# A two-branch layer kernel: the next block's x loads issued two phase rotations sooner

**Chip, cores, metric.** One core of a Trainium2 chip. The experiments ran in five rounds on five chips (the record numbers them 0, 6, 8, 9 and 12); ratios compare kernels within a round. The metric is device microseconds (us) of one execution, median of several runs; lower is better.

## The reference, cut

`out = x + A(layernorm(x)) + B(layernorm(x))` for 2048 rows of 1024 numbers in bfloat16. A is a linear recurrence over the rows with complex states; B is a dense layer of width 3584 with the activation `h * tanh(softplus(h))` between two matrix products.

```python
    x = A_x
    xn = _layernorm(x, axis=-1)
    return x + _A_ref(xn, ...) + _B_ref(xn, B_w1, B_b1, B_w2)   # arguments cut
```

## The kernel before

The rows go through in four blocks of 512. In each block the TensorE makes 28 tiles of the first dense layer (one PSUM bank each, eight banks in turn), then eight pairs of projections into the recurrence, then the tail (the second dense layer and the recurrence's output). The weights pass through a ring of SBUF slots, which SyncE refills in pairs. The VectorE copies each tile out of its bank and does, in the same in-order queue, everything else that is small: among it, in the first block, the layer norm statistics of the *next* block. In the first block GpSimd also makes the phases of the rotation table, eight rotations of three operations. The next block's x is loaded by GpSimd from the middle of these.

```python
    def load_x(queue, blk, q):                      # 128 rows, 256 KB
        r0 = blk * TB + q * P
        i = blk % 2
        queue.dma(lambda e: e.dma_start(xx[:, i, q, :], A_x[0, r0:r0 + P, :]), ...)   # cut

    def ln_stats_only(blk, q):                      # VectorE; waits for the load
        ...
            vop(lambda e, h=h: e.bn_stats(stats[:, s, h, :], xx[:, i, q, h * 512:(h + 1) * 512]), ...)
        vop(lambda e: e.bn_aggr(mv[:, q, :], stats[:, s, :, :]), ...)

    for j in range(NJ):                             # GpSimd
        phases(j)                                   # rotation j: px, py, ph
        if j == 3:
            for q in range(NQ):
                load_x(PO, 1, q)

    def first_tile(blk, f):
        bank, hs = f % 8, f % (2 * GF)
        ...                                         # 8 matmuls into the bank; weights from the ring
        if f % 4 == 3:
            item_done()                             # SyncE loads two more ring slots
            item_done()
        if f % GF == 0 and f >= 2 * GF:
            mish_mul(f // GF - 2)                   # VectorE group multiply, at f = 14 and 21
        vop(lambda e: e.tensor_scalar(hb[:, hs, ts], ps[:, bank, ts], b1(f), None, op0=ALU.add), ...)

        def side(f):                                # after first_tile(blk, f); here the first block
            ...                                     # cut
            if f in (14, 16, 18, 20):
                ln_stats_only(1, (f - 14) // 2)
            if f < 24 and f % 3 == 2:
                transpose_B(f // 3)                 # SyncE, the same in-order queue as the ring
```

Of the kernel before, what the change touches and what calls it, by code (L numbers as in the profile page):

```python
# [135 lines left out]
def bass_parallel_sum__ssm_conv_s5__dense_activation_mish__prompt_kernel(  # L136
    nc: bass.Bass,
    A_x: bass.AP,
    A_Lambda_re: bass.AP,
    A_Lambda_im: bass.AP,  # L140
    A_B_re: bass.AP,
    A_B_im: bass.AP,
    A_C_re: bass.AP,
    A_C_im: bass.AP,
    A_log_dt: bass.AP,
    A_Dskip: bass.AP,
    B_x: bass.AP,
    B_w1: bass.AP,
    B_b1: bass.AP,
    B_w2: bass.AP,  # L150
    out: bass.AP,
):
    build_kernel(nc, A_x, A_Lambda_re, A_Lambda_im, A_B_re, A_B_im, A_C_re, A_C_im,
                 A_log_dt, A_Dskip, B_w1, B_b1, B_w2, out)


def build_kernel(nc, A_x, A_Lambda_re, A_Lambda_im, A_B_re, A_B_im, A_C_re, A_C_im,
# [149 lines left out]
    def load_x(queue, blk, q):  # L307
        r0 = blk * TB + q * P
        i = blk % 2
        queue.dma(lambda e: e.dma_start(xx[:, i, q, :], A_x[0, r0:r0 + P, :]),  # L310
                  s_xx[i][q] if blk else s_x0[q], writes=[b_xx[i][q]])
# [310 lines left out]
    def phases(j):  # L622

        xs, b_xs = ph_slot(j)
        pop(lambda e: e.tensor_scalar(px[:], iot[:], cj("thp", j), None, op0=ALU.mult),  # L625
            reads=[b_iot, b_cs["thp"]], writes=[b_px])
        pop(lambda e: e.tensor_scalar(py[:], px[:], ROUND_MAGIC, -ROUND_MAGIC, op0=ALU.add, op1=ALU.add),  # L627
            reads=[b_px], writes=[b_py])
        pop(lambda e: e.tensor_tensor(xs[:], px[:], py[:], op=ALU.subtract),  # L629
            reads=[b_px, b_py], writes=[b_xs])  # L630
# [45 lines left out]
    turns()  # L676
    for j in range(NJ):
        phases(j)
        if j == 3:
            for q in range(NQ):  # L680
                load_x(PO, 1, q)

# [299 lines left out]
```

## Time and profile before

| | before |
|---|---|
| timed, first set of runs | 620.77 us (620.40 to 621.11) |
| the profiled execution | 623.69 us, span 622.4 us |
| TensorE | 99% busy |
| VectorE, ScalarE, GpSimd | 75%, 40%, 9% |

The table by stretches of this profile says where the TensorE is idle. Its columns are the stretch, its length, then busy us (and instructions) of TensorE, weight loads, VectorE, ScalarE and GpSimd, the granted clock, the DMA share and GB/s.

```profile
0.00:22.24 22.24, 20.46 (x194) 17.90 (x194) 16.45 (x49) 9.40 (x17) 8.15 (x22) 1.00 0.98 258
22.24:60.55 38.31, 38.30 (x178) 17.02 (x175) 34.12 (x66) 32.85 (x23) 36.47 (x26) 1.00 1.08 270
60.55:62.35 1.80, 0.00 (x1) 0.01 (x1) 1.69 (x3) 1.77 (x3) 1.80 (x1) 1.00 1.30 331
```

Two places: some 1.8 us in the start, which the change doesn't touch, and one stop of 1.80 us in which the VectorE is the one that works. The DMA engines are full (share about 1) in all three.

### The profile page before, as it was taken

Reading aid. Unit: us, or ns where it says so; the run is one execution under the profiler, and the core shown is the slowest. Engines: PE = TensorE matmul, PEld = TensorE weight load, DVE = VectorE, ACT = ScalarE, POOL = GpSimd, SP = SyncE. Lnnn points to the kernel's source line nnn. Section 1 sums busy time; section 2 is a strip of 40 time slices with the busy share of each in tenths; the row PEclk is TensorE's granted clock in tenths of the full one; section 3 lists DMA queues with packets and bytes.
Section 4 is the critical chain, followed back from the end, with each engine's and each line's share of the span. In section 5 each row is a group of like instructions: output and inputs, shape, how many; then the busy total and the mean of one; then the engine's idle time right before and its main releaser. Section 6 shows DMA issues by size and latency. Waiting matters only on the chain.

```text
span 622.4 us, 7428 instructions
## 1 busy us (share of the span) xinstructions
PE 616.7 (99%) x2959; PEld 288.3 (46%) x2959; DVE 468.1 (75%) x698; ACT 248.1 (40%) x161; POOL 54.5 (9%) x57
## 2 busy tenths in 40 slices
PE   8998999999999999999999999999999999999998
PEld 7643444444444444444444444444444444444444
DVE  6988999999557599999047759999624856999603
ACT  4589997332069950000008992000000999000000
POOL 2899200000100000000010000000000000000000
DMA  9999995850355400774054430276302541033001
GB/s 230 298 263 280 224 145 176 199 167 0 117 173 174 144 2 9 218 185 131 11 188 138 135 136 1 73 203 173 93 35 101 164 174 69 1 119 118 1 0 68
DMA packets 97918, 79.94 MB, mean 128 GB/s; under 512 B 51035, under 2 KB 80347, under 8 KB 97883
## 3 DMA queue, kind: packets, MB, share of 16 engines
q1 hardware_dynamic: 94384, 72.17, 41.4%
q0 software_dynamic: 960, 3.15, 1.8%
q10 hardware_dynamic: 2538, 4.14, 1.8%
q8 instruction: 24, 0.39, 0.3%
q14 instruction: 12, 0.09, 0.1%
HBM read 63.19 MB, written 4.19 MB: 108 GB/s over the span
## 4 chain that ended last, share of the span: by engine, by line
PE 90%; POOL 4%; DMA 2%; DVE 2%; issue 1%; SPq 0%; POOLq 0%; DVEq 0%
PE ps L825 49%; PE ps L745 23%; PE ps L767 18%; DMA xx<-in_A_x_dram 2%; POOL py L627 1%; POOL px L625 1%; POOL ph_h L629 1%; DVE stats L449 1%; POOL rb L568 1%; DVE hb L754 1%; DVE act L730 0%; PE ps L839 0%; DVE stats L371 0%; SPq L310 0%; SPq L343 0%
## 5 line engine op out<-in xcount | busy, mean ns | idle before, releaser
L825 PE MATMUL ps<-ring,act 128*128 128x512 bf16 x896 | 194.0, 379 | 0.0
L745 PE MATMUL ps<-xnT,ring 128*128 128x512 bf16 x840 | 182.1, 379 | 0.0
L723 ACT ACTIVATE act<-hb 128x3584 bf16<-128x3584 bf16 x16 | 50.9, 3183 | 220.6 <-DVE hb L754 220.1
L825 PEld LDWEIGHTS ps<-ring,act 128*128 128x128 bf16 x896 | 87.7, 98 | 105.7
L745 PEld LDWEIGHTS ps<-xnT,ring 128*128 128x128 bf16 x840 | 82.1, 98 | 99.2 <-DVE hb L754 0.7
L754 DVE TENSOR_SCALAR hb<-ps,par 128x512 bf16<-128x512 f32 (+1 forms) x112 | 80.0, 730 | 52.6 <-PE ps L745 51.7
L767 PE MATMUL ps<-xnT,BT 128*128 128x512 bf16 x512 | 111.3, 379 | 1.8 <-DVE hb L754 1.8
L825 PE MATMUL ps<-CT,hT 128*128 128x512 bf16 x506 | 109.9, 379 | 0.0
L772 DVE TENSOR_TENSOR mt<-ps,tab 128x1024 bf16<-128x1024 f32 x64 | 75.4, 1219 | 13.3 <-PE ps L767 11.7
L767 PEld LDWEIGHTS ps<-xnT,BT 128*128 128x128 bf16 x512 | 50.0, 98 | 62.5 <-DVE hb L754 2.3
L825 PEld LDWEIGHTS ps<-CT,hT 128*128 128x128 bf16 x506 | 49.5, 98 | 59.7
L790 DVE TENSOR_TENSOR_SCAN hT<-cs,qi,hT 128x512 bf16<-128x512 f32 x48 | 58.9, 1269 | 0.0
L870 DVE TENSOR_TENSOR xx<-ps,xx 128x1024 bf16<-128x1024 f32 (+1 forms) x16 | 18.8, 1190 | 45.6 <-PE ps L825 45.6
L725 ACT ACTIVATE act<-act 128x3584 bf16<-128x3584 bf16 x16 | 51.1, 3191 | 0.2
L724 ACT ACTIVATE act<-act 128x3584 bf16<-128x3584 bf16 x16 | 51.0, 3190 | 0.2
L795 DVE TENSOR_TENSOR mt<-hT,tab 128x1024 bf16<-128x1024 bf16 x64 | 41.4, 688 | 1.1
L730 DVE TENSOR_TENSOR act<-act,hb 128x3584 bf16<-128x3584 bf16 x16 | 34.0, 2127 | 1.3 <-ACT act L725 1.3
L310 POOL DMA_DIRECT2D xx<-in_A_x_dram x12 | 6.7, 562 | 250.2 <-DVE xx L870 245.8
L699 ACT ACTIVATE ct<-CT,cs 128x512 f32<-128x512 bf16 x16 | 11.5, 720 | 26.3 <-DVE CT L701 25.9
L725 ACT ACT_TABLE_LOAD x16 | 20.5, 1283 | 0.3
L724 ACT ACT_TABLE_LOAD x16 | 20.5, 1283 | 0.3
L449 DVE BATCH_NORM_STATS2 stats<-xx 128x6 f32<-128x512 bf16 x24 | 16.3, 679 | 3.7 <-DMA xx<-in_A_x_dram 3.3
(101 smaller groups left out, 297.9 us busy)
## 6 DMA issues: line engine op xcount, KB each, us to landing
ring<-in_B_w_dram SPq DMA_DIRECT2D x112, 512.0 KB, 4.1
out_dram<-xx ACTq DMA_DIRECT2D x15, 256.0 KB, 2.0
xx<-in_A_x_dram POOLq DMA_DIRECT2D x12, 256.0 KB, 4.2
xx<-in_A_x_dram SPq DMA_DIRECT2D x3, 256.0 KB, 4.7
xx<-in_A_x_dram SPq DMA_DIRECT2D x2, 128.0 KB, 2.3
dsk<-in_A_Dskip_dram SPq DMA_DIRECT2D x1, 256.0 KB, 5.1
xnT<-xn SPq DMA_TRANSPOSE x14, 4.5
BT<-in_A_B_re_dram SPq DMA_TRANSPOSE x8, 5.8
```

The lines of the kernel that those rows point to most:

```text
L449: vop(lambda e, h=h: e.bn_stats(stats[:, s, h, :], xx[:, i, q, h * 512:(h + 1) * 512]), reads=[b_xx[i][q]], writes=[b_stats[s]])
L723: aop(lambda e: e.activation(a, hs, AF.Exp), reads=[b_hb[g % 2]], writes=[b_act[g]])
L724: aop(lambda e: e.activation(a, a, AF.Ln, bias=1.0), reads=[b_act[g]], writes=[b_act[g]])
L725: aop(lambda e: e.activation(a, a, AF.Tanh), reads=[b_act[g]], writes=[b_act[g]])
L730: vop(lambda e: e.tensor_tensor(a, a, hs, op=ALU.mult), reads=[b_act[g], b_hb[g % 2]], writes=[b_act[g]])
L745: PE.mm(lambda e, k=k, w=w: e.matmul(ps[:, bank, :], lhsT=w, rhs=xnT[:, k, :], start=k == 0, stop=k == NK - 1), reads=[b_ring[s]] + b_xnT, ...
L754: vop(lambda e: e.tensor_scalar(hb[:, hs, ts], ps[:, bank, ts], b1(f), None, op0=ALU.add), reads=[b_ps[bank], b_par], writes=[b_hbf[hs]])
L767: PE.mm(lambda e, j=j, ci=ci, k=k, bank=bank: e.matmul(ps[:, bank + ci, :], lhsT=BT[:, ci, j, k, :], rhs=xnT[:, k, :], start=k == 0, stop= ...
L772: vop(lambda e, s=s, u=u, j=j: e.tensor_tensor(mt[:, s, :, :], u, tab[:, s, j, :].unsqueeze(1).to_broadcast([P, 2, TB]), op=ALU.mult), rea ...
L790: vop(lambda e, ci=ci, init=init: e.tensor_tensor_scan(out=hT[:, ci, j, :], data0=cj("r", j).to_broadcast([P, TB]), data1=hT[:, ci, j, :], ...
L795: vop(lambda e, s=s: e.tensor_tensor(mt[:, s, :, :], hT[:, :, j, :], tab[:, s, j, :].unsqueeze(1).to_broadcast([P, 2, TB]), op=ALU.mult), ...
L825: PE.mm(lambda e: e.matmul(ps[:, u, :], lhsT=lhsT, rhs=rhs, start=st_, stop=last), reads=reads, writes=[b_ps[u]], first=st_, last=last)
```

## The change

Its intent: x of the next block lands before the VectorE asks for it, so that the VectorE never waits and frees the PSUM banks in time.

```diff
     for j in range(NJ):
         phases(j)
-        if j == 3:
+        if j == 1:
             for q in range(NQ):
                 load_x(PO, 1, q)
```

## The prediction

> **What bounds the kernel now.** I read the page first, for the bound and for the chain of waits; then the timeline of the TensorE around the first block, to find where it really stands still; then the timeline of the VectorE back from that stop, and the GpSimd's timeline and the DMA issues for what set off the wait.
>
> ```profile
> PE 616.7 (99%) x2959; PEld 288.3 (46%) x2959; DVE 468.1 (75%) x698; ACT 248.1 (40%) x161; POOL 54.5 (9%) x57
> ...
> PE 90%; POOL 4%; DMA 2%; DVE 2%; issue 1%; SPq 0%; POOLq 0%; DVEq 0%
> ```
>
> The TensorE is busy for 616.7 of 622.4 us, so all its idle time together is 5.7 us. The chain gives 4% to GpSimd and 2% to DMA, some 37 us, but that is not what a change there can win: the chain only says whom the last released instruction waited for, and while it runs through GpSimd and a transfer the TensorE is still working. What can be won is the time in which the TensorE stands still:
>
> ```profile
> 22.24 36.58 PE L745 MATMUL ps<-xnT,ring 128*128 128x512 bf16 x168
> 58.66 1.89 PE L767 MATMUL ps<-xnT,BT 128*128 128x512 bf16 x8
> 62.35 7.94 PE L767 MATMUL ps<-xnT,BT 128*128 128x512 bf16 x36 [1.80 <-DVE hb L754]
> ```
>
> 168 matmuls in 36.42 us are 217 ns each, and in the later stages the chain has 352 in 75.97 us, 216 ns each: the TensorE runs at its full pace up to 60.55 us, stops once for 1.80 us, and runs through to the end. In the list of waits from 22 to 64 us that is its only matmul wait; the weight loads have 0.7 us more in two waits for the same VectorE line. The stop is for a PSUM bank: the second projection tile writes bank 5, which tile 21 of the first layer used, and the VectorE has not copied tile 21 out. Why it is late stands in its timeline:
>
> ```profile
> 41.33 2.71 DVE L730 TENSOR_TENSOR act<-act,hb 128x3584 bf16<-128x3584 bf16 x1
> 44.14 0.75 DVE L754 TENSOR_SCALAR hb<-ps,par 128x512 bf16<-128x512 f32 x1
> 47.41 1.43 DVE L449 BATCH_NORM_STATS2 stats<-xx 128x6 f32<-128x512 bf16 x2 [2.51 <-DMA xx<-in_A_x_dram]
> 48.87 0.21 DVE L451 BATCH_NORM_AGGREGATE mv<-stats 128x2 f32<-128x12 f32 x1
> 48.99 1.36 DVE L754 TENSOR_SCALAR hb<-ps,par 128x512 bf16<-128x512 f32 x2
> 51.12 1.42 DVE L449 BATCH_NORM_STATS2 stats<-xx 128x6 f32<-128x512 bf16 x2 [0.78 <-DMA xx<-in_A_x_dram]
> ...
> 58.40 3.03 DVE L730 TENSOR_TENSOR act<-act,hb 128x3584 bf16<-128x3584 bf16 x1
> 61.54 2.07 DVE L754 TENSOR_SCALAR hb<-ps,par 128x512 bf16<-128x512 f32 x3
> ```
>
> The VectorE takes its work in order. After tile 14 it wants the statistics of the next block's x, whose first two quarters have not landed: it waits 2.51 and 0.78 us, 3.29 us together. Apart from that it is full. Tile 21 comes out of its copy at 62.30 us; the TensorE wanted the bank at 60.55. The x loads are late because GpSimd issues them only after four phase rotations:
>
> ```profile
> 31.41 1.57 POOL L625 TENSOR_SCALAR px<-iot,cs 128x512 f32<-128x512 f32 x1
> ...
> 40.89 1.27 POOL L629 TENSOR_TENSOR ph_h<-px,py 128x512 f32<-128x512 f32 x1
> 42.10 2.35 POOL L310 DMA_DIRECT2D xx<-in_A_x_dram  x4
> ```
>
> The listing of that load's line in this stretch gives 5.3 us from issue to landing for the first, then 8.3, 8.7 and 8.9 us. The DMA engines are full meanwhile: the table by stretches has a DMA share of 1.09 from 31.31 to 42.10 us, 1.09 to 53.98 and 1.11 to 62.35.
>
> **What the Trainium skill says.** "SBUF — State Buffer", section "Who interferes with whom": VectorE and GpSimd share a port pair that one instruction holds for its whole length, and a VectorE instruction with two SBUF inputs contends with a GpSimd instruction that reads SBUF. The trace agrees in kind: the 128x3584 multiply takes 2.71 and 3.03 us beside GpSimd and 2.02 us at 92.20, where GpSimd is done. The same page, "A bandwidth-pool intuition that's wrong (but worth ruling out)", warns that a load issued by GpSimd can lack its descriptors while the VectorE holds that pair. Here the issues took 0.54 to 0.75 us each although the multiply ran from 41.33 to 44.04, so no such starvation shows. "DMA: Bandwidth & Descriptors", section "Anatomy of one DMA — SWDGE (gpsimd) path", fits 2.0 us plus bytes/436e3 for such a load: 2.6 us for 256 KB. The trace has 5.3 to 8.9 us, so here the queueing behind weights and transposes decides; the measurement stands. The same page, "Issuing engines are not separate DMA queues", says all issuers share 16 DMA engines: the loads will not be free at their new place either.
>
> **The change part by part.** No instruction is added or removed. Four issues (2.35 us of GpSimd) move ahead of phase rotations 2 and 3.
>
> Loads: the second rotation ends at 31.31 us, so the issues lie at about 31.4 to 33.7 instead of 42.1 to 44.4, 10.8 us earlier. With the same transfer times of 5.3 to 8.9 us they land at about 36.7 to 42 us; double the longest and the last is there at about 51. The VectorE asks for the quarters at 44.9, and, without waits, at about 48, 51 and 53.7. All of its 3.29 us of waiting go.
>
> GpSimd: rotations 2 and 3 end 2.35 us later, at about 38.9 and 44.5; from the fifth on nothing moves, since the same work lies before it. ScalarE reads rotation 2 at 59.0 and rotation 3 at 61.05. This costs nothing.
>
> VectorE: tile 14 is out at 44.89. Then statistics and tiles follow without a gap, and the multiply moves from 58.40 to 58.40 − 3.29 = 55.1 us. It needs the tanh of its group, which ScalarE ends at 53.64: still 1.5 us of room. Tile 21 is out at 62.30 − 3.29 = 59.0 us. The TensorE wants its bank at 60.55: 1.5 us of room. The stop of 1.80 us is gone, and half of what the VectorE gains is slack.
>
> Behind it: the first projection result is read by the VectorE after tile 27, at 66.15 − 3.29 = 62.9, when the TensorE ends it at about 62.1 and its table is long there (57.1). ScalarE's activations keep their times, because they wait for each other and not for x: the last tanh of this block ends at 96.88. The multiply behind it, at 98.51 now, can move up only to that, about 1.6 us. So the VectorE keeps 1.6 us of its 3.29 there while the TensorE runs 1.8 us earlier. That 0.2 us comes out of the slack before the last part of the block: the last scaled C rows are ready at 156.4 us, and their first use is 16 matmuls before the tail's end at 164.39, at about 160.9, so 4.5 us. From the second block on, everything hangs on the TensorE and moves with it.
>
> Sum: −1.80 us, and perhaps −0.2 us more from the two weight-load waits. 620.77 − 1.80 = 618.97 us, or −0.3%. The timed runs lie below the profiled one (620.77 against 623.69), and I can't see how much of the stop they have; so I take a little less than the full gain, 619.2 us.
>
> **The rivals.** (1) The weights become late. The x loads now compete with ring loads and transposes issued from 31 to 42 us. SyncE issues in order, and between 42 and 53 us, beside the x loads, a transpose issue took 4.10 us and two weight issues 2.59 instead of about 1.06: some 3 us of delay, which would now come earlier. The ring pair issued at 41.98 is the nearest: it landed after 5.9 and 8.6 us, and its first half is used by tile 24 at about 52.6 us. Issued at 45 with 5.9 us it lands at 51. That is close, but each us late would cost at most one. The other way round, the lighter traffic after 42 us helps it. Eating the whole gain needs 3.4 us more than this; time 619 to 621.
>
> (2) The stop is not in the timed runs, because it is recording that slows the transfers. Then the VectorE has slack already and nothing is gained: 620.8. For it speaks that the stop is only 1.80 of 3.29 us of waiting, so transfers 2 us quicker would remove it; against it that the DMA engines are full anyway.
>
> (3) The VectorE loses as much as it wins: the group multiply at 41.33 then lies beside the fourth rotation, which reads SBUF, and not beside the issues. At most it grows from 2.71 to about 3.03 us, as its fellow at 58.40 has it: 0.3 us of 1.5 us of room. No effect.
>
> (4) The wait is only replaced by another in front of the same bank, the tanh of the group or a table. The tanh has 1.5 us of room, the table 5.8 us.
>
> **Range and chances.** The ceiling is what the TensorE stands still from 22 us on: 1.8 us and a few tenths, so 618.4 is about the best. The floor is no gain, 620.77. 2% are 12.4 us, over twice the TensorE's whole idle time, so faster by over 2% can't be; slower by over 2% would need a wait of 12 us that no figure here suggests.
>
> **What would show it.** In the changed trace: the four issues at about 31.4 us; no VectorE wait for x before the statistics; the multiply at about 55.1 us; tile 21 out at about 59; TensorE matmuls without a stop near 60.5 and the first tail starting at about 86.6 instead of 88.42; rotation 3 ending near 44.5. The prediction is wrong if a TensorE wait for the ring shows near 52 us, if the VectorE waits for a tanh at 53.6, or if the stop is gone and the timed runs are no shorter.

## The result, and the profile after

621 us before, 621 us after: 620.96 us (620.60 to 621.53, 6 runs) against 620.95 us (620.40 to 621.67, 6 runs), ratio 1.0001, 95% interval 0.9988 to 1.0014. A ratio here is the mean time of one kernel's fast runs over that of the other's of the same rounds, so not quite the ratio of the medians that are quoted. The time lies outside the predicted range of 618.4 to 620.8.

The profile after, however, looks as promised. First the page's busy line and its chain of waits:

```profile
PE 613.2 (99%) x2903; PEld 288.2 (46%) x2959; DVE 467.0 (75%) x698; ACT 247.4 (40%) x161; POOL 55.1 (9%) x57
...
PE 97%; DMA 1%; issue 1%; SPq 1%; DVE 0%
```

The chain no longer runs through GpSimd and x. (It has 56 matmul records fewer than before, not 56 matmuls.) The TensorE's timeline of the first block, after:

```profile
22.07 36.21 PE L745 MATMUL ps<-xnT,ring 128*128 128x512 bf16 x164
58.11 12.25 PE L767 MATMUL ps<-xnT,BT 128*128 128x512 bf16 x55
```

The stop is gone. The timelines of GpSimd and the VectorE, after:

```profile
30.86 2.36 POOL L310 DMA_DIRECT2D xx<-in_A_x_dram  x4
...
42.79 1.84 POOL L629 TENSOR_TENSOR ph_h<-px,py 128x512 f32<-128x512 f32 x1
```

```profile
41.49 2.02 DVE L730 TENSOR_TENSOR act<-act,hb 128x3584 bf16<-128x3584 bf16 x1
43.61 0.75 DVE L754 TENSOR_SCALAR hb<-ps,par 128x512 bf16<-128x512 f32 x1
44.28 1.41 DVE L449 BATCH_NORM_STATS2 stats<-xx 128x6 f32<-128x512 bf16 x2
...
54.39 2.22 DVE L730 TENSOR_TENSOR act<-act,hb 128x3584 bf16<-128x3584 bf16 x1
56.72 4.70 DVE L754 TENSOR_SCALAR hb<-ps,par 128x512 bf16<-128x512 f32 x7
```

No bracket stands behind the statistics any more: the VectorE doesn't wait for x. Tile 21 is out at about 57.5 us, and its bank is wanted at about 59.8. The span is 619.8 us, 2.6 us less than the profile of before. So the two profiles differ by what was predicted, and the timed runs don't differ. Either the timed runs of before never had the stop, or those of after lose it again somewhere.

### The profile page after: what moved, and what is told of

Its sections match the earlier page's. It is cut to its first block, busy times and chain, and to the rows that moved or that the text cites. A ratio compares the mean times of both kernels' runs of the same rounds, so it can differ in the third digit from the quotient of the medians.

```text
span 619.8 us, 7372 instructions
## 1 busy us (share of the span) xinstructions
PE 613.2 (99%) x2903; PEld 288.2 (46%) x2959; DVE 467.0 (75%) x698; ACT 247.4 (40%) x161; POOL 55.1 (9%) x57
## 4 chain that ended last, share of the span: by engine, by line
PE 97%; DMA 1%; issue 1%; SPq 1%; DVE 0%
PE ps L825 49%; PE ps L745 29%; PE ps L767 18%; DMA ring<-in_B_w_dram 1%; PE ps L558 1%; PE ps L549 0%; SPq L310 0%; PE ps L839 0%; PE ps L401 0%; SPq L343 0%; SPq L314 0%; DVE xx L893 0%
## 5 line engine op out<-in xcount | busy, mean ns | idle before, releaser
L754 DVE TENSOR_SCALAR hb<-ps,par 128x512 bf16<-128x512 f32 (+1 forms) x112 | 79.9, 729 | 52.6 <-PE ps L745 51.7
L870 DVE TENSOR_TENSOR xx<-ps,xx 128x1024 bf16<-128x1024 f32 (+1 forms) x16 | 18.8, 1189 | 44.6 <-PE ps L825 44.5
L795 DVE TENSOR_TENSOR mt<-hT,tab 128x1024 bf16<-128x1024 bf16 x64 | 41.4, 688 | 1.1
L730 DVE TENSOR_TENSOR act<-act,hb 128x3584 bf16<-128x3584 bf16 x16 | 32.5, 2034 | 3.0 <-ACT act L725 3.0
L790 DVE TENSOR_TENSOR_SCAN hT<-cs,hT 128x512 bf16<-128x512 f32 x16 | 18.7, 1208 | 0.0
```

The source lines that it names most:

```text
L730: vop(lambda e: e.tensor_tensor(a, a, hs, op=ALU.mult), reads=[b_act[g], b_hb[g % 2]], writes=[b_act[g]])
L790: vop(lambda e, ci=ci, init=init: e.tensor_tensor_scan(out=hT[:, ci, j, :], data0=cj("r", j).to_broadcast([P, TB]), data1=hT[:, ci, j, :], ...
L795: vop(lambda e, s=s: e.tensor_tensor(mt[:, s, :, :], hT[:, :, j, :], tab[:, s, j, :].unsqueeze(1).to_broadcast([P, 2, TB]), op=ALU.mult), ...
L870: vop(lambda e: e.tensor_tensor(xr, src, xr, op=ALU.add), reads=b_ps[bank:bank + n] + [b_x], writes=[b_x])
```

## The experiments

Theory A: the profile was of an unusually long execution (623.69 us), and the 1.80 us stop belongs to such ones only. Theory B: the stop is in all runs of before, and the change gives it back elsewhere. Others came up on the way, and the expectations name them: C (a late start), D (a new wait, for weights or transposes) and E (a cause that both kernels share).

### Both kernels again: b_again, a_again

No edit; one new profile and six times each.

> The kernel before, unchanged, profiled and timed again. Theory A (the 1.80 us stop was of the profiled execution, which took 623.69 us against 620.4 to 621.67 timed): the new profile spans about 619.5 us, with no TensorE stop near 60 us and the VectorE waiting for x for under 1.5 us in all. Theory B (the stop is in the timed runs too, and the change gives 1.8 us back somewhere else): the new profile again has a stop of about 1.8 us near 60 us, at a time of about 621. Ratio 1.000 in both; its interval is the noise of the comparison.

> The changed kernel again, for a second profile and a narrower interval. Theory A: no TensorE stop from 22 us on, as in the first profile, ratio 1.000 within 0.1%. Theory B: in some executions a stop or a later start that costs 1.8 us, to be seen in this profile or as a spread of the times; ratio 1.000 too.

Measured: b_again 620.97 us (ratio 0.9989, interval 0.9967 to 1.0011), a_again 621.15 us (0.9996, 0.9972 to 1.0019); the shared 11 runs of before, 621.17 us. The new profile of the kernel before, timelines of the TensorE and of the VectorE:

```profile
21.27 36.21 PE L745 MATMUL ps<-xnT,ring 128*128 128x512 bf16 x164
57.31 17.86 PE L767 MATMUL ps<-xnT,BT 128*128 128x512 bf16 x81
```

```profile
44.63 1.42 DVE L449 BATCH_NORM_STATS2 stats<-xx 128x6 f32<-128x512 bf16 x2 [0.96 <-DMA xx<-in_A_x_dram]
...
54.75 1.97 DVE L730 TENSOR_TENSOR act<-act,hb 128x3584 bf16<-128x3584 bf16 x1
```

The same program, no stop: it waits 0.96 us for x, not 3.29, and its second group multiply takes 1.97 us, not 3.03. Its first two x loads took 3.7 and 5.0 us to land, against 5.3 and 8.3. Theory A holds for this execution.

### The loads later still: x4, x5

```diff
-        if j == 3:
+        if j == 4:      # x5: if j == 5
```

> The x loads one rotation (5.05 us by the trace of before) later than before. In the profile of before the VectorE waited 3.29 us for x and had 1.49 us of room, so the stop is the wait less 1.49. Theory A: the timed runs of before have no stop, so some of the 5.05 us is swallowed: 3.5 to 5.0 us slower, 624.5 to 626.0. Theory B: the stop is there already, so all of it shows: 5.05 us slower, 626.0.

> The x loads two rotations (10.1 us) later than before. Both theories: 5.05 us over the kernel with one rotation, slope one. Theory A: 8.5 to 10.0 us slower than before, 629.5 to 631. Theory B: 10.1 us slower, 631.

Measured: x4 629.03 us (ratio 1.0113), x5 633.98 us (1.0184). The step from x4 to x5 is 4.95 us, near the 5.05 expected; the first step is 8 us, more than either theory allowed. The profile of x4, the TensorE's timeline and the table by stretches, says why:

```profile
54.45 11.03 PE L745 MATMUL ps<-xnT,ring 128*128 128x512 bf16 x39 [5.44 <-DVE hb L754]
```

```profile
48.90:54.45 5.55, 0.11 (x1) 0.00 (x1) 2.27 (x5) 5.51 (x4) 5.34 (x6) 0.79 1.03 344
54.45:58.50 4.05, 4.05 (x10) 1.50 (x11) 3.98 (x7) 3.92 (x7) 3.86 (x3) 0.50 1.07 234
```

Two terms were missing from the expectation. The issue came at 47.75 us, 6.9 us after that of b_again and not 5.05, because the first operation of rotation 4 now met the group multiply and took 3.22 us instead of 1.58; the wait for x was 8.27 us. And after a stop of 5.44 us the TensorE's granted clock is 0.50 in the next 4 us. From its first full-width tile to its first projection x4 takes 43.89 us (21.43 to 65.32), b_again 36.04: 7.85 us more, of which 5.44 are the stop and 2.4 the lost clock. (The 39 matmuls of the line can't be counted for this, since some records are missing.) The Trainium skill, "TensorE: Matmul & The Clock Gate", section "What's actually happening", states half the clock after an idle window of about 3.4 us; this trace agrees, and the stops of 1.80 us in before and 2.70 us in b_st2 below left the clock at 1.00. The useful number is the room: x4 waited 8.27 us and stopped 5.44, x5 waited 14.29 and stopped 11.46, so 2.83 us of wait cost nothing in both (here the bank of tile 15 is the one that runs out first). An ordinary wait of about 1 us lies well inside.

### Taking the room away: b_st2, a_st2

```diff
             if f in (14, 16, 18, 20):
                 ln_stats_only(1, (f - 14) // 2)
+            if f == 20:
+                ln_stats_only(1, 3)
+                ln_stats_only(1, 3)
```

> The kernel before, with the statistics of the last quarter computed two more times (2 x 1.57 us of VectorE, same result) ahead of the group multiply. It uses up the room before tile 21's bank. Theory A (an ordinary execution of before has room left, 1.46 us beside a wait for x of 0.96 us): stop of 3.14 - 1.46 = 1.7 us, 622.7 us. Theory B (the timed runs of before already have a 1.8 us stop): all 3.14 us show, 624.1 us.

> The changed kernel with the same added statistics. Theory A (the change does free the VectorE of its wait for x, about 1 us in an ordinary execution, and only has no use for it): room of 59.84 - 57.4 = 2.4 us, stop of 0.7 us, 621.7 us, 1.0 us faster than b_st2. Theory B (the change frees the VectorE of nothing in timed runs, or it is taken back by the shared port): no difference from b_st2.

Measured: b_st2 624.08 us (ratio 1.0054, 1.0030 to 1.0078), a_st2 621.59 us (1.0010, 0.9998 to 1.0022). The TensorE's timelines, b_st2 and then a_st2:

```profile
52.68 6.22 PE L745 MATMUL ps<-xnT,ring 128*128 128x512 bf16 x28 [0.81 <-DMA ring<-in_B_w_dram]
58.73 1.89 PE L767 MATMUL ps<-xnT,BT 128*128 128x512 bf16 x8
63.32 12.04 PE L767 MATMUL ps<-xnT,BT 128*128 128x512 bf16 x55 [2.70 <-DVE hb L754]
```

```profile
60.38 14.85 PE L767 MATMUL ps<-xnT,BT 128*128 128x512 bf16 x68 [0.64 <-DVE hb L754]
```

With its room used up, the kernel before is 2.49 us slower than the changed one. The stop of a_st2 was expected at 0.7 us and is 0.64. So the change does free the VectorE, as intended, and only lacks a use for it. The difference was expected at 1.0 us: the profiled b_st2 waited 2.7 us for x and 0.81 us for ring weights, which nobody had in the sum. For b_st2 alone theory B had the better number (624.1, against 622.7 by theory A), but by the profile for another reason: these two waits, and added statistics that took 3.4 us (the multiply at 60.43 instead of 57.02) and not 3.14. That the unprofiled runs of b_st2 were alike isn't shown. Theory B is out by the difference of the pair, which it had at nothing: what it calls given back is there for the taking.

### More profiles of both: b_p2, a_p2, a_p3, b_p3, a_p4, a_p5

No edit. The times of over 622.5 us, seen in both kernels by now, needed a profile.

> One more profile of the kernel before. Theory A: if its time is about 621, no stop near 60 us and a wait for x under 2.4 us; if it is about 623, a stop of about 2 us with a wait for x of 3 us or a group multiply of 3 us. Theory C (the times of about 623 come from the start of the kernel, not from the stop): a late start of the full-width tiles (over 23 us) and no stop.

> One more profile of the changed kernel. Theory A: no stop whatever its time; if its time is about 623 the extra lies before 31 us, where the change does nothing. Theory D: in a long execution a new wait (ring or transposes) shows between 31 and 60 us.

> The changed kernel again, for how often it has long executions (over 622.5 us: so far 8 of 35 timed runs of before, 1 of 13 of after). Theory A (the long executions of before are those with the stop): at most 1 of 6 here, the median about 620.9 as ever. Theory E (they have a cause that both kernels share, such as the start or the ring): 1 or 2 of 6, as in before.

> The kernel before again. Both theories: 1 or 2 of 6 over 622.5 us and 2 or 3 of the 11 shared ones. If its profile falls on one of them, theory A wants a stop of about 2 us near 60 us and a wait for x of over 2.4 us or a group multiply of 3 us; theory E wants a late start or a wait for the ring, with no stop near 60 us.

> As the changed kernel above. Theory A: at most 1 of 6 over 622.5 us. Theory E: 1 or 2 of 6.

> As the changed kernel above. Theory A: at most 1 of 6 over 622.5 us, and 0 to 2 of the 18 of these three. Theory E: 4 of the 18.

Measured: b_p2 620.92, a_p2 620.64 (one run each, so of unknown state, at a clock of 1.00); a_p3 621.18, b_p3 621.59, a_p4 621.23, a_p5 621.08 us (ratios 1.0005, 1.0007, 1.0001, 0.9994). By luck the profiled run of b_p3 was a long one, 623.78 us. Its TensorE and VectorE timelines:

```profile
22.70 31.04 PE L745 MATMUL ps<-xnT,ring 128*128 128x512 bf16 x141
54.15 5.35 PE L745 MATMUL ps<-xnT,ring 128*128 128x512 bf16 x23 [0.41 <-DVE hb L754]
...
62.54 12.69 PE L767 MATMUL ps<-xnT,BT 128*128 128x512 bf16 x57 [1.31 <-DVE hb L754]
```

```profile
47.77 1.42 DVE L449 BATCH_NORM_STATS2 stats<-xx 128x6 f32<-128x512 bf16 x2 [2.65 <-DMA xx<-in_A_x_dram]
51.81 1.42 DVE L449 BATCH_NORM_STATS2 stats<-xx 128x6 f32<-128x512 bf16 x2 [1.10 <-DMA xx<-in_A_x_dram]
```

There are the two waits and the stop of the first profile again. All profiles of the two kernels side by side, in us; time and trace of a row are of the same execution, "begin" is the first full-width tile. "Ring room" is worked out: from the landing of the ring pair's first half (issue plus time to landing) to its first use, taken as begin plus 140 matmuls of 0.2158 us.

| execution | time | begin | wait for x | stop | time − begin | ring room |
|---|---|---|---|---|---|---|
| before, first | 623.69 | 22.24 | 3.29 | 1.80 | 601.45 | 4.6 |
| b_again | 620.27 | 21.27 | 0.96 | 0 | 599.00 | 3.7 |
| b_p2 | 620.92 | 21.60 | 0.85 | 0 | 599.32 | 4.9 |
| b_p3 | 623.78 | 22.70 | 3.75 | 1.72 | 601.08 | 4.9 |
| after, first | 621.08 | 22.07 | 0 | 0 | 599.01 | 1.2 |
| a_again | 621.30 | 22.20 | 0 | 0 | 599.10 | 3.5 |
| a_p2 | 620.64 | 21.33 | 0 | 0 | 599.31 | 2.7 |
| a_p3 | 620.38 | 21.28 | 0 | 0 | 599.10 | 3.3 |
| a_p4 | 621.26 | 22.17 | 0 | 0 | 599.09 | 3.7 |
| a_p5 | 621.07 | 21.98 | 0 | 0 | 599.09 | 3.3 |

What an ordinary execution takes is its begin plus 599.0 to 599.3 us, in both kernels. The spread of the ordinary times is the spread of the start (21.3 to 22.2 us). The two executions with a stop have 2.0 to 2.5 us more, a few tenths over the stop itself. Theory A is shown for before; why x lands late in some executions stays open. The last column is the other side: in the changed kernel the ring pair has less room, in one case 1.2 us.

Long times did not vanish with the change, though. 15 of 74 timed runs of before were over 622.5 us, and 3 of 31 of after, but those three were 623.23, 624.11 and 625.53 us, and the means are 621.37 and 621.38 us. By these counts alone a smaller share in after isn't shown (one-sided exact test: 0.15); of the 18 runs of a_p3 to a_p5 it was 2, where theory A had 0 to 2 and theory E 4. None of the three left a profile, but the record has their mean granted clock: 0.997 in two (623.23 and 625.53 us), and 1.000 in all 15 long runs of before. Since the stops of 1.80 and 1.72 us left it at 1.00, these two were probably something else; what, stays open. Even if the change took all of the long times away, it would win some 0.4 us of the mean (an estimate: 15 of 74 times 2 us), less than the interval of the first comparison can show.

### Full DMA engines on purpose: b_tr, a_tr, b_tr2, a_tr2

```diff
+        if g == 0 and not traffic:       # behind ScalarE's first exponential (tr)
+            spare_load(2)                # 256 KB of x into an unused part of CT
+        if g == 0 and len(traffic) == 2: # behind its first tanh (tr)
+            spare_load(4)
```

The comments are added and the helper `spare_load` is cut. In b_tr2 and a_tr2 instead four such loads behind the second exponential.

> The kernel before with six spare 256 KB loads (result unused and right) that ScalarE issues in the first block, two at about 30 us and four at about 39 us: full DMA engines, as an unlucky execution has them. Theory A: x lands 1 to 4 us later, the VectorE's wait passes its room of about 2.4 us, stop of 1 to 3 us, 622 to 624 us. Theory E (x's landing does not decide): no stop, 621 us.

> The changed kernel with the same spare loads. Theory A: x has landed by then or does at about 40 us, no stop, 621 us, 1 to 3 us faster than b_tr. Theory D (the change has put x in front of the weights, and its own long executions are waits for the ring pair issued at about 46 us): a TensorE wait for the ring near 52 us of 1 to 4 us, no faster than b_tr.

> The kernel before with four spare 256 KB loads that ScalarE issues at about 41.4 us (behind its second exponential), so beside the x loads. Theory A: x lands 1 to 4 us later than in an ordinary execution, the wait passes its room of 2.4 us, stop of 1 to 3 us, 622 to 624 us. If the ring pair issued at about 42 us suffers too: up to 2 us more.

> The changed kernel with the same spare loads at about 41.4 us. Its x has landed at 39 to 40 us. Theory A alone: no stop, 621 us. Theory D: the ring pair's first half, issued at about 44 to 46 us with 1.2 to 3.7 us of room, is pushed 2 to 4 us back: a wait for the ring near 52 us of 0 to 2.5 us, 621 to 623.5 us.

Measured: b_tr 622.08 us (ratio 1.0024, 0.9996 to 1.0051), a_tr 625.05 us (1.0064, 1.0041 to 1.0087); b_tr2 622.69 us (620.62 to 629.01; ratio 1.0049, 1.0013 to 1.0085), a_tr2 623.66 us (621.11 to 632.79; fast runs alone: median 622.88, ratio 1.0038, 1.0003 to 1.0074). In the first pair the spare loads were issued from 26.7 and 34.4 us on, sooner than meant, since ScalarE's queue runs ahead of its computing; so they lay beside the x loads of the changed kernel, and the kernel before waited only 1.6 us for x. The TensorE's timeline of a_tr:

```profile
46.12 7.08 PE L759 MATMUL ps<-xnT,ring 128*128 128x512 bf16 x32 [1.19 <-DMA ring<-in_B_w_dram]
55.09 6.22 PE L759 MATMUL ps<-xnT,ring 128*128 128x512 bf16 x27 [1.89 <-DMA ring<-in_B_w_dram]
```

Two waits for weights, where b_tr has one of 0.99 us. The changed kernel is 2.97 us the slower by the medians, but the intervals of the two ratios overlap, so the slower isn't shown by the times. In the second pair the loads lay at 40 to 43 us, beside x of the kernel before, which then waited 2.65 us for x in its profile, just within its room (no matmul stop). The profiled run of a_tr2 is in the slow state: two waits for the ring of 3.76 and 3.47 us, its x loads 6.3 to 12.5 us in flight, and the granted clock falling (mean 0.80 over the next 8.7 us) only after the first stop. It is one execution and proves no rate; the fast medians of this pair are 0.2 us apart with ranges of about 8 us each, so that pair is inconclusive on which kernel bears it better. Theory A alone (no stop at all in the changed kernel) is wrong; theory D, a wait for the ring, is seen in a_tr.

### A place between: x2

```diff
-        if j == 3:
+        if j == 2:
```

> The middle way: x loads one rotation sooner than before, one later than after (issue at about 36 us), without spare loads. Should keep the VectorE from waiting (x there at about 41 to 45 us, wanted at 43.7 to 44.9). All theories: median 620.9 as both kernels, for nothing stops in an ordinary execution; theory D lets one hope for fewer long executions, 0 or 1 of 6 over 622.5 us.

Measured: 621.78 us (620.70 to 625.32; ratio 1.0013, 0.9989 to 1.0036), two of six over 622.5 us. No gain. But its profile, of a run of 622.19 us without any spare load, has the ring wait of theory D in the TensorE's timeline:

```profile
48.84 3.40 PE L745 MATMUL ps<-xnT,ring 128*128 128x512 bf16 x15
53.09 3.19 PE L745 MATMUL ps<-xnT,ring 128*128 128x512 bf16 x13 [0.85 <-DMA ring<-in_B_w_dram]
```

The ring pair was issued at 48.1 us, where before issues it at 41.4 to 42.3, and landed 5.0 us later, just when the TensorE goes on. So x loads issued sooner than before can hold back the weights, in an execution nobody disturbed. But the changed placement isn't needed for such a wait. b_st2, which is the kernel before up to its added statistics (the first at 57.15 us), has one of 0.81 us in the timeline above: its ring pair was issued at 42.94 us, little later than usual, but just behind x, and its first half took 9.7 us to land, to 52.6. How often either kernel waits so isn't known, nor whether the three long runs of after did. No version here beats both kernels.

## Why the prediction was wrong

- **The step that failed** is the last of the working, "Sum: −1.80 us", carried to the timed runs as "620.77 − 1.80 = 618.97". The 1.80 us were read rightly from the trace, but the trace was of a long execution. In the two ordinary profiles of before the wait for x is 0.96 and 0.85 us instead of 3.29, and the stop is 0. The term is nothing in ordinary runs, by their times 59 of 74.
- **The sign was on the page:** 623.69 us profiled against at most 621.11 timed. The prediction saw it and took off only 0.2 us. The whole gain (1.80) was smaller than this gap (2.6), so the stop could lie inside it.
- **The sign it had set itself,** "the stop is gone and the timed runs are no shorter", is what came.
- **Rival (2)** named the outcome, 620.8 us and no gain, but with the wrong reason. It isn't that recording slows transfers: the other profiles of before are recorded too, and two of three have no stop. Executions of one program differ, and the profile can fall on any.
- **The room** was underrated. The first profile gave 3.29 − 1.80 = 1.49 us of wait without a stop, because there the group multiply also took 3.03 us beside GpSimd; with the ordinary 1.97 us it is 1.49 + 1.06 = 2.55. b_tr2 waited 2.65 us without a matmul stop.
- **Right:** the issue time (31.4, measured 30.86), rotation 3 ending near 44.5 (44.63), no wait for x, the multiply at 55.1 (54.39), no stop near 60.5, the tail at about 86.6 (85.74). Tile 21 was expected at 59.0 and came at 57.5, since both group multiplies were shorter (2.02 and 2.22 us for 2.71 and 3.03; rival (3) had expected growth) and the start was earlier. Their length follows from how far GpSimd's two-input operation of 1.27 us (`ph<-px,py`) is when the multiply begins: 0.12 us into it 3.03 us, 0.44 us 2.71, 0.60 us (b_p3) 2.54, 0.93 us (after) 2.22, and 1.97 to 2.02 where none is under way. So this room, too, hangs on the moment.
- **Rival (1),** late weights, was set at a delay of some 3 us of the ring pair; it was issued 1.7 to 4.1 us later (43.7 to 46.1 for 42.0). In ordinary executions this costs nothing, as said. It is what the change pays in return: ring room of 1.2 to 3.7 us instead of 3.7 to 4.9 in the profiles of the table. b_st2 shows that the kernel before can lose this room too: by the same sum it has -0.9.
- **Range:** its upper end, 620.8, was the median of three runs of before. The median of all 74 is 621.00, so even "no gain" lay outside it. The end should have held the noise of the baseline.

## What to carry to other kernels

Before a stop in a trace is priced, hold the traced execution's own time against the timed runs: where it is longer by more than the stop is worth, trace again, for the stop may be what made it long. A wait costs only what exceeds the room behind it, and the room can be measured by adding work until it shows. And where the DMA engines are full, an earlier load is paid for by whatever it overtakes: look for the next transfer's deadline too.

## What the Trainium skill lacked or had wrong

- "DMA: Bandwidth & Descriptors", section "Anatomy of one DMA — SWDGE (gpsimd) path": its fit gives 2.6 us for 256 KB. Beside full DMA engines (share 1.06 to 1.09) the same four loads of the same program took 3.6 to 9.2 us over four profiles of the kernel before. The page gives no time for a load that queues behind others, nor a spread.
- No page that I read says that executions of one unchanged kernel can differ by whole waits: 15 of 74 runs were over 622.5 us with a median of 621.00, and a profile is of one execution (two of four profiles of before were long ones, with waits for x of 3.29 and 3.75 us against 0.96 and 0.85).
